# Rows of two time blocks accumulated by state group in four PSUM tiles, one spectrum overlapped on VectorE, one input tile without its TensorE fix-up, and three scans' scaled states on ScalarE

## The chip, the cores and the metric

The kernel runs on one core of a Trainium2 chip. The metric is the device time of one execution in microseconds (us); lower is better. The engines that matter are TensorE (PE in the profile: matrix products into PSUM), VectorE (DVE), ScalarE (ACT), GpSimd (POOL, which here issues the DMAs that add what they carry to their destination) and SyncE (SP, which issues the plain loads, the transposing loads and the stores). Each engine works through its own list of instructions in order.

## What is computed

Two sequence mixers over the same `x` (2048 steps, 1024 channels) are blended by a gate. Cut to what matters:

```
g  = sigmoid((x * gate_w).sum(-1))
# A: diagonal complex state space, 1024 states
h[t] = Lam_bar * h[t-1] + B_bar x[t];   a = 2 Re(C h) + x * Dskip
# B: short filter over k, times v, then a long convolution
kv = shift(k) * v;   y = irfft(rfft(kv) * rfft(ssm_k)) + kv * ssm_D;   b = x * y
out = g * a + (1 - g) * b
```

`x` and all weights are bf16, the output is bf16.

## The kernel before

**First half, the convolution (to about 217 us).** Channels are taken in eight chunks `c` of 128. For a chunk, `fwd_K` (line 542) makes the spectrum of the filter and `fwd_V` (558) that of the data by matrix products with cosine and sine tables, ScalarE moves both from PSUM to SBUF (`Kh`, `Vh` in the profile), `products` (571) multiplies them on VectorE into `G`, and `inverse` (621) turns `G` back on TensorE (`psz`) and sends the result to a scratch in DRAM (`cv_scr`). The sequence is cut into four blocks; in `fwd_K` each block's spectrum gets the spectrum of the block before it added by 16 matmuls of 384 columns in all (lines 553 to 555).

**Second half, the states.** Time is cut into four blocks `tb` of 512 steps, states into four groups `g` of 256. `Bu(i)` (686) is the input product of the pair `order[i] = (tb, g)`, in two halves of 16 matmuls of 512 columns. A pair is either *plain* (`Bu_plain`, 736; the product of even and odd steps, `both` in the profile) or a *tile* (`Bu_tile`, 710; `odd` and `even` apart, with `lamd` matmuls that add Lambda times the odd half). For a plain pair `turn_U` (752) does that addition later: six ScalarE instructions into two `Q` tiles and two adding DMAs from POOL. Some input products are already mixed into the first half (the generator `tiles`, line 961).

`scan` (763) is VectorE's part for one pair: scan number `j = 4 tb + g`. It rotates the input (`A`, `trn`), runs four scan instructions (`W`), rotates back (`hb`, the odd-step states), then makes `q = lam * hb` (line 811, four scalings) and adds it to `U` (lines 813 to 815, the even-step states). `advance(j)` (1191) runs the middle of scan `j`, the first instruction of scan `j+1`, then the end of scan `j`; a `product` is done in the middle, after the second `trn`.

An output *row* `k` is a tile of 128 steps (`k = 4 tb + tl`). `loads(k)` (827) fetches the convolution's result `pbb` and `x` (`xr`); `scale_b(k)` (841) scales `pbb` by `1-g` on ScalarE, makes `gd = g * Dskip` there, and POOL adds `gd` to `pbb` by DMA; `product(k)` (875) multiplies `xr` by `pbb` on VectorE; `Cy` (1164) is the output product, 32 matmuls of 512 columns over all four groups in one PSUM tile (`psy`), followed by `scale_a` (869) on ScalarE; `combine(k)` (879) is an adding DMA of `xr` into that result, and `store(k)` (882) sends it out. PSUM is a ring of four tiles of 4 KB per partition.

**What sets the order.** Everything is emitted by hand, and `put` (92) keeps each engine's instructions in the order in which they are emitted. For each scan `j` the loop (1209) emits, in turn: the loads due, `advance(j)`, the VectorE part of the C matrix's scaling, the first half of a `turn_U`, the units of `plan[j]` (line 1174: `B9` is an input product, `C4` a row), the second half of that `turn_U`, and a `scale_b`. After the loop rows 12 to 15 are accumulated group by group, with group 3 last.

Of the kernel before, what the change touches and what calls it, by code (L numbers as in the profile page):

```python
# [20 lines left out]
def kernel(  # L21
# [75 lines left out]
    def mm(o, l, r, first, last):  # L97
        put("pe", nc.tensor.matmul, o, lhsT=l, rhs=r, start=first, stop=last)
# [18 lines left out]
    def act(o, i, **kw):  # L117
        put("act", nc.scalar.activation, out=o, in_=i, **kw)
# [423 lines left out]
    def fwd_K(c, fis=range(NFI)):  # L542
        eo = eos["k", c]
        if c not in KH:
            KH[c] = spectrum("K", c)
        for fi in fis:
            fsl = slice(fi * 128, (fi + 1) * 128)
            ps = ps2([128, 2, 4, 128], "psk")
            for cc in range(2):
                tab = CF if cc == 0 else SF  # L550
                for mt in range(2):
                    mm(ps[:, cc], tab[:, mt, fsl], eo[:, cc, mt], mt == 0, False)
                for mt in range(2):
                    tb2 = (SF, NCF)[cc][:, mt, fsl]
                    mm(ps[:, cc, 1:4], tb2, eo[:, 1 - cc, mt, 0:3], False, mt == 1)
            act(of_tile(KH[c], fi), ps, func=ACT.Copy)

    def fwd_V(c, fis=range(NFI)):
        eo = eos["v", c]
# [126 lines left out]
    def Bu(i):  # L686
        tb, g = order[i]
        if i in (10, 11):
            if i == 10:
                s5p["u2"] = xt_pool.tile([128, 2, 2 * (4 * HB + 4)], BF16, name="U2", tag="xT")  # L690
            U = s5p["u2"][:, i - 10]
        else:
            shape = [128, 2 * (4 * HB + 4)]
            if i in (6, 7, 8, 15):
                U = u4(shape, BF16, "U")
            else:
                home = uu[0 if i in (0, 1, 13, 14) else 1] if i < 6 or i in (13, 14) else s5p["uu"]
                U = home.tile(shape, BF16, name="U")
        if i in (4, 5, 7) or i >= 8:
            V_, O_ = U[:, 0:4 * HB], U[:, 4 * HB:]  # L700
            V_ = V_.rearrange("p (c j t) -> p c j t", c=2, j=2)
            O_ = O_.rearrange("p (c j t) -> p c j t", c=2, j=2)
            Us[tb, g] = V_, O_[:, :, :, 2:]
            turns_U[i] = turn_U(g, V_, O_)
            return [Bu_plain(tb, g, V_, O_, j) for j in range(2)]
        U = U[:, 0:8 * HB].rearrange("p (a c j t) -> p a c j t", a=2, c=2, j=2)
        Us[tb, g] = U[:, 0], U[:, 1]
        return [Bu_tile(tb, g, U, j, (i, j) == (2, 1)) for j in range(2)]
# [43 lines left out]
    def turn_U(g, V_, O_):  # L752
        both = slice(0, 2)
        for part in (((both, both, lam[:, 0]),), ((0, 1, lam[:, 1]), (1, 0, mlam))):
# [5 lines left out]
            gather(V_, Q)  # L760
            yield

    def scan(tb, g, fin):


        last = tb == NTB - 1 and g == NG - 1
        Ve, Uo = Us[tb, g]
        A = w2([128, 2, 2, HB], BF16, "A")
        W = None

        for js in ([slice(0, 1), slice(1, 2)] if last else [slice(0, 2)]):
            g2 = slice(2 * g + js.start, 2 * g + js.stop)
            full = [128, 2, js.stop - js.start, HB]
            Aj, Uj = A[:, :, js], Ve[:, :, js]
            tt(Aj, bc(TC[:, g2][:, None], full), Uj, ALU.mult)
            if js.start == 0:
                yield
            b = w2([128, 2, 2, HB], BF16, "trn")[:, :, js]
            tt(b, bc(TS[:, g2][:, None], full), Uj, ALU.mult)
            if js.start == 0:  # L780
                if g == 0 and tb > 0:
                    carry(tb)
                step(fin)
            tt(Aj[:, 0], Aj[:, 0], b[:, 1], ALU.add)
            tt(Aj[:, 1], Aj[:, 1], b[:, 0], ALU.subtract)
            if W is None:
                W = w2([128, 2, 2, HB], BF16, "W")
            for j in range(js.start, js.stop):
                pi = 2 * g + j
                for c in range(2):  # L790
                    put("dve", V.tensor_tensor_scan, out=W[:, c, j], data0=bc(rv2[:, pi:pi + 1], [128, HB]),
                        data1=A[:, c, j], initial=0.0 if tb == 0 else init[tb][:, c, pi:pi + 1],
                        op0=ALU.mult, op1=ALU.add)
            if js.start == 0:
                run(fin)
                hbs[tb, g] = s5p["hb"].tile([128, 2, 2, HB], BF16, name="hb")
            hb = hbs[tb, g][:, :, js]
            Wj = W[:, :, js]
            tt(hb, bc(TC[:, g2][:, None], full), Wj, ALU.mult)
            if tb < NTB - 1:  # L800
                copy(WL[tb][:, :, g2], Wj[:, :, :, HB - 1])
            b = w2([128, 2, 2, HB], BF16, "trn")[:, :, js]
            tt(b, bc(TS[:, g2][:, None], full), Wj, ALU.mult)
            if not last:
                yield
            tt(hb[:, 0], hb[:, 0], b[:, 1], ALU.subtract)
            tt(hb[:, 1], hb[:, 1], b[:, 0], ALU.add)
            q = [w2([128, 2, 2, HB], BF16, "q") for k in range(2)]
            for k in range(2):
                for j in range(js.start, js.stop):  # L810
                    ts(q[k][:, :, j], hbs[tb, g][:, :, j], lam[:, k, 2 * g + j:2 * g + j + 1], None, ALU.mult)
            o, (q1, q2) = Uo[:, :, js], [x[:, :, js] for x in q]
            tt(o, o, q1, ALU.add)
            tt(o[:, 0], o[:, 0], q2[:, 1], ALU.subtract)
            tt(o[:, 1], o[:, 1], q2[:, 0], ALU.add)

    ios, gas = {}, {}

# [8 lines left out]
    def loads(t_):  # L827
        if t_ >= NT - 4:
            if t_ == NT - 4:
                ios["last"] = xt_first.tile([128, 4, D], BF16, name="xlast", tag="xT")  # L830
            pbb, xr = bt_row(1, t_ - NT + 4), ios["last"][:, t_ - NT + 4]
        elif t_ in (3, 4, 8, 9):
            pbb, xr = (bt_row(0, 2 * ((t_ - 3) % 5) + k) for k in range(2))
        else:
            pbb = s5p["io"].tile([128, D], BF16, name="pbb", bufs=3)
            xr = s5p["io"].tile([128, D], BF16, name="xr", bufs=3)
        move(pbb.rearrange("p (c d) -> p c d", d=128), cv_scr[:, :, t_ % 4, t_ // 4].rearrange("c p d -> p c d"))
        move(xr, rows_of(xf, t_))
        ios[t_] = pbb, xr
# [70 lines left out]
    def run(gen):  # L910
        for _ in gen:
            pass
# [50 lines left out]
    for c in range(NC - 1):  # L963
# [66 lines left out]
        step(prod)  # L1030
        run(fk)
        run(prod)
        if nn < NC:
            tv = times_v(nn)
            step(tv)
        bu = [next(tiles) for _ in range({1: 1, 2: 1, 3: 1, 5: 1, 6: 2}.get(c, 0))] + [none, none]
        if c == 5:
            bu[1] = ahead = next(tiles)
        step(bu[0])
# [10 lines left out]
        fwd_V(n, (2, 3))  # L1050
        if bu[1] is not ahead:
            step(bu[1])
        if c == 2:
            lam_diag(1, lam_pool)
        old = tabs
# [43 lines left out]
    with tc.tile_pool(name="fin", bufs=1, side="right") as fin:  # L1099
# [7 lines left out]
        run(old)  # L1107
        steps(prod, 3)
        run(back)
        b0, b1, b2, b3 = tiles  # L1110
        run(b0)
        gate(1)
        run(b1)
        run(prod)
        lam_diag(2, lam_pool, True)
        run(b2)
        run(b3)
        gate(2)
        b6, b7 = Bu(6)
        step(b6)  # L1120
        steps(turning[0], 2)
        step(b7)
        step(b6)
        back = inverse(c)
        step(back)
        step(b7)
        run(back)
        steps(turning[1], 2)
    h3.close()
# [41 lines left out]


    NS = NTB * NG
    plan = ["B8", "B9 B10", "B11", "B12 C0", "C1", "C2", "C3", "B13 B14", "C4 B15", "C5", "C6", "C7", "C8", "C9", "C10", "C11"]
    turned = dict(zip(range(3, 12), (8, 9, 4, 10, 11, 12, 13, 14, 15)))
    turned[0] = 7
    rows = dict(scaled=0)

    def between(j):
        for unit in plan[j].split():  # L1180
            if unit[0] == "C":
                product(int(unit[1:]))
        yield

    def prepare():
        scale_b(rows["scaled"])
        rows["scaled"] += 1

    scans = [scan(j // NG, j % NG, between(j)) for j in range(NS)]

# [4 lines left out]
        run(scans[j])  # L1195

    def Cy_row(k):
        if k + 3 < NT - 4:
            loads(k + 3)
        if k > 0:  # L1200
            store(k - 1)
        Cy(k // NG, k % NG)
        combine(k)
        if 0 < k < NT - 6:
            prepare()

    Bu_next(7)
    step(scans[0])
    for j in range(NS):
        if 10 <= j < 14:  # L1210
            loads(j + 2)
        advance(j)
        for t in turning[2 * j:2 * j + 2]:
            run(t)
# [1 line left out]
        turn = turns_U[turned[j]] if j in turned else none  # L1216
        step(turn)
        for unit in plan[j].split():
            (Bu_next if unit[0] == "B" else Cy_row)(int(unit[1:]))
        run(turn)  # L1220
        if j == 5:
            run(turns_U[5])
        if j < 3:
            prepare()
        if 11 <= j < 15:
            scale_b(j + 1)
        if j == 0:
            load_xT(3)
            loads(2)
        if j == 8:  # L1230
            gate(3)

    store(NT - 5)
    tb = NTB - 1
    t0 = tb * 4
    pss = []
# [44 lines left out]
```

## Time and profile before

| | |
|---|---|
| median of 3 runs | 399.38 us (399.07 to 400.0) |
| the profiled execution | 399.34 us, of which the span of the core is 397.3 us |
| granted TensorE clock | 0.997 |
| TensorE | 387.4 us busy (97% of the span), 2493 matmuls |
| VectorE | 378.3 us (95%), 616 instructions |
| ScalarE | 279.4 us (70%), 420 instructions |
| GpSimd | 70.8 us (18%), 95 instructions |

Times inside the profile count from the start of the span; the 2.0 us between span and run lie around it. Nearly every instruction stands under line 94, the line of `put`, so the groups are read by the names of the tiles: `psy<-CT,hb` is an output product, `xr<-xr,pbb` and `BT<-BT` (128x1024, VectorE) are products of rows for rows whose two buffers lie in the spent matrix `BT` (3, 4, 8 and 9).

### The profile page before, as it was taken

What the parts mean: (1) busy time and instruction counts of PE and PEld (TensorE: products, weight loads), DVE (VectorE), ACT (ScalarE), POOL (GpSimd) and SP (SyncE); (2) the same over time, 40 slices, a digit from 0 to 9 for tenths busy, and PEclk for the clock granted to TensorE, in tenths of its full rate; (3) what the DMA queues carried; (4) which work ended last, traced back from release to release, by engine and by line L of the source; (5) the groups of instructions that cost most, each with busy time, mean ns of one, the idle gap of its engine ahead of it and who ended that gap; (6) DMA issues with size and microseconds to landing.
All of it is one profiled execution on the core that took longest, in us unless ns stands there. A gap on an engine that the chain in (4) does not pass through costs nothing.

```text
span 397.3 us, 6652 instructions
## 1 busy us (share of the span) xinstructions
PE 387.4 (97%) x2493; PEld 210.8 (53%) x2493; DVE 378.3 (95%) x616; ACT 279.4 (70%) x420; POOL 70.8 (18%) x95
## 2 busy tenths in 40 slices
PE   8999899999999999999999999999999999999995
PEld 5456357474656648567557444444444444444442
DVE  8799999999999999999999999999999999999974
ACT  4797995979879796765455689957995668974001
POOL 3011030200303011020000001413442333541000
PEclk9999999999999999999999999999999999999998
DMA  7869996996929389068994699898999869998302
GB/s 160 160 139 209 204 221 131 222 225 126 222 52 226 68 150 196 27 134 108 173 204 102 166 171 229 166 197 157 217 183 193 178 146 203 245 244 202 75 26 106
DMA packets 129313, 65.19 MB, mean 164 GB/s; under 512 B 106361, under 2 KB 113281, under 8 KB 129282
## 3 DMA queue, kind: packets, MB, share of 16 engines
q1 hardware_dynamic: 117664, 42.22, 48.8%
q0 software_dynamic: 11536, 22.55, 33.2%
q8 instruction: 19, 0.31, 0.3%
q14 instruction: 12, 0.10, 0.1%
q10 hardware_dynamic: 82, 0.02, 0.0%
HBM read 12.86 MB, written 8.39 MB: 53 GB/s over the span
## 4 chain that ended last, share of the span: by engine, by line
PE 82%; DVE 9%; ACT 6%; issue 2%; POOL 0%; DVEq 0%; POOLq 0%; ACTq 0%
PE psy L94 28%; PE both L94 19%; PE psk L94 9%; PE psz L94 5%; PE taps L94 5%; PE even L94 5%; PE odd L94 4%; DVE BT L94 3%; PE psv L94 3%; PE foldk L94 3%; ACT Vh L94 2%; DVE wkh L94 2%; DVE G L94 1%; PE p L94 1%; DVE t L94 1%
## 5 line engine op out<-in xcount | busy, mean ns | idle before, releaser
L94 PEld LDWEIGHTS <-BT 128*128 128x128 bf16 x672 | 65.4, 98 | 45.2
L94 PE MATMUL both<-xT,BT 128*128 128x512 bf16 x352 | 76.8, 379 | 0.0
L94 PE MATMUL psy<-CT,hb 128*128 128x512 bf16 x256 | 56.6, 379 | 0.0
L94 PE MATMUL psy<-CT,U 128*128 128x512 bf16 x256 | 56.4, 379 | 0.0
L94 PEld LDWEIGHTS <-U 128*128 128x128 bf16 x256 | 25.0, 98 | 30.2
L94 PEld LDWEIGHTS <-hb 128*128 128x128 bf16 x256 | 25.0, 98 | 30.0
L94 ACT ACTIVATE Vh<-psv 128x1024 bf16<-128x1024 f32 x32 | 31.0, 1034 | 11.5 <-PE psv L94 11.5
L94 ACT ACTIVATE U<-both 128x512 bf16<-128x512 f32 x44 | 24.2, 594 | 17.3 <-PE both L94 17.2
L94 POOL DMA_DIRECT2D U<-Q x22 | 19.2, 942 | 89.7 <-ACT U L94 51.8
L94 DVE TENSOR_TENSOR_SCAN W<-rv,init,A 128x256 bf16<-128x256 f32 x48 | 32.2, 732 | 0.0
L94 PE MATMUL taps<-dg,kT 128*128 128x128 bf16 x512 | 31.0, 222 | 0.0
L94 POOL DMA_DIRECT2D G<-wkh x8 | 9.7, 1218 | 115.7 <-DVE wkh L94 115.7
L94 PEld LDWEIGHTS <-kT 128*128 128x128 bf16 x512 | 29.6, 99 | 1.0 <-DMA kT<-in_B_k_dram 0.3
L94 PE MATMUL psk<-eok,SF 128*128 128x512 bf16 (+1 forms) x128 | 29.4, 352 | 0.0
L94 PEld LDWEIGHTS <-SF 128*128 128x128 bf16 x192 | 18.8, 98 | 19.9 <-issue 0.8
L94 PE MATMUL psz<-G,CI 128*128 128x512 bf16 x64 | 24.3, 380 | 2.4 <-DVE G L94 1.9
L94 ACT ACTIVATE BT<-psy,gcols 128x1024 bf16<-128x1024 f32 x5 | 5.6, 1114 | 29.9 <-PE psy L94 29.9
L94 ACT ACTIVATE Q<-U,lam 128x512 bf16<-128x512 bf16 (+1 forms) x44 | 25.5, 607 | 0.0
L94 PE MATMUL psz<-G,SI 128*128 128x512 bf16 x64 | 24.3, 379 | 0.0
L94 DVE TENSOR_TENSOR U<-U,q 128x512 bf16<-128x512 bf16 (+2 forms) x51 | 23.5, 488 | 0.6
L94 DVE TENSOR_TENSOR wkh<-BT,Vh 128x3072 bf16<-128x3072 bf16 (+4 forms) x20 | 21.8, 1111 | 0.0
L94 DVE TENSOR_TENSOR wkh<-Kh,Vh 128x3072 bf16<-128x3072 bf16 (+2 forms) x16 | 21.3, 1352 | 0.0
(179 smaller groups left out, 776.4 us busy)
## 6 DMA issues: line engine op xcount, KB each, us to landing
U<-Q POOLq DMA_DIRECT2D x22, 256.0 KB, 5.0
G<-wkh POOLq DMA_DIRECT2D x6, 768.0 KB, 7.8
cv_scr<-cv SPq DMA_DIRECT2D x16, 256.0 KB, 2.8
v<-in_B_v_dram SPq DMA_DIRECT2D x3, 1024.0 KB, 9.8
pbb<-cv_scr SPq DMA_DIRECT2D x8, 256.0 KB, 4.7
xr<-in_A_x_dram SPq DMA_DIRECT2D x8, 256.0 KB, 4.6
pbb<-gd POOLq DMA_DIRECT2D x8, 256.0 KB, 6.6
BT<-cv_scr SPq DMA_DIRECT2D x8, 256.0 KB, 6.6
```

Of the source, the lines that this page charges most:

```text
L94: i = f(*a, **kw)
```

## The change

Four things are changed together.

1. *Last kernel spectrum.* For chunk 7 `fwd_K` leaves out the 16 matmuls of 384 columns, and `overlap_K` does the same six additions in place on VectorE, after the products of chunk 6.
2. *Pair 6 plain.* Pair 6 (block 0, group 2) becomes plain. Its eight `lamd` matmuls and the table `lamd2` (six ScalarE instructions) go; a `turn_U(6)` comes, run whole just ahead of input product 7. One half of pair 4 moves from the last chunk's stage to the end of the stage before it.
3. *Rows of blocks 1 and 2 by groups.* `Cy_group(tb, g)` does group `g` of all four rows of a block, in four PSUM tiles that are held through the four groups. The plan, the loads, the scalings of `pbb`, the products and the stores have new due times.
4. *q by ScalarE.* For scans 12, 13 and 14 the four scalings of `q` become ScalarE instructions, emitted at the end of iteration `j` ahead of its `scale_b`; the three additions to `U` follow in the next scan, after its scan instructions.

```diff
@@ fwd_K
-                    mm(ps[:, cc], tab[:, mt, fsl], eo[:, cc, mt], mt == 0, False)
-                for mt in range(2):
+                    mm(ps[:, cc], tab[:, mt, fsl], eo[:, cc, mt], mt == 0, c == NC - 1 and mt == 1)
+                for mt in range(0 if c == NC - 1 else 2):
...
+    def overlap_K(c):
+        K = KH[c][0]
+        for b in (3, 2, 1):
+            tt(K[:, 0, b], K[:, 0, b], K[:, 1, b - 1], ALU.add)
+            tt(K[:, 1, b], K[:, 1, b], K[:, 0, b - 1], ALU.subtract)
@@ Bu
-        if i in (4, 5, 7) or i >= 8:
+        if i in (4, 5) or i >= 6:
@@ scan
+            while put_off:
+                put_off.pop()[1]()
             if js.start == 0:
                 run(fin)
...
-            q = [w2([128, 2, 2, HB], BF16, "q") for k in range(2)]
-            ...
+            by_act = tb == NTB - 1 and not last
+            if by_act:
+                q = [s5p["Q"].tile([128, 2, 2, HB], BF16, name="Q") for k in range(2)]
+            else:
+                q = [w2([128, 2, 2, HB], BF16, "q") for k in range(2)]
+            def scaled(q=q):
+                for k in range(2):
+                    for j in range(js.start, js.stop):
+                        a = (q[k][:, :, j], hbs[tb, g][:, :, j], lam[:, k, 2 * g + j:2 * g + j + 1])
+                        if by_act:
+                            act(a[0], a[1], func=ACT.Identity, scale=a[2])
+                        else:
+                            ts(*a, None, ALU.mult)
+            def summed(q=q, js=js):
+                ...
+            if by_act:
+                put_off.append((scaled, summed))
@@ loads
-        elif t_ in (3, 4, 8, 9):
+        elif t_ in (3, 4, 8):
...
+        elif t_ in (9, 10):
+            if t_ == 9:
+                ios["two"] = xt_pool.tile([128, 4, D], BF16, name="xtwo", tag="xT")
+            pbb, xr = (ios["two"][:, 2 * (t_ - 9) + k] for k in range(2))
@@ stage of chunk 6 (c == 6, n == 7) and last stage
         run(prod)
+        if n == NC - 1:
+            overlap_K(n)
...
-        bu = [next(tiles) for _ in range({1: 1, 2: 1, 3: 1, 5: 1, 6: 2}.get(c, 0))] + [none, none]
+        bu = [next(tiles) for _ in range({1: 1, 2: 1, 3: 1, 5: 1, 6: 3}.get(c, 0))] + [none, none]
...
+        run(bu[2] if c == 6 else none)
...
-        b0, b1, b2, b3 = tiles
+        b0, b1, b2 = tiles
...
-        lam_diag(2, lam_pool, True)
         run(b2)
-        run(b3)
         gate(2)
         b6, b7 = Bu(6)
-        step(b6)
+        run(b6)
         steps(turning[0], 2)
-        step(b7)
-        step(b6)
+        run(b7)
         back = inverse(c)
@@ the loop over scans
-    plan = ["B8", "B9 B10", "B11", "B12 C0", "C1", "C2", "C3", "B13 B14", "C4 B15", "C5", "C6", "C7", "C8", "C9", "C10", "C11"]
+    plan = ["B8", "B9 B10", "B11", "B12 C0", "C1", "C2", "C3 B13", "B14 B15", "G10", "G11", "G12 G13", "G20", "G21",
+            "G22 G23", "", ""]
...
+    multiplied = {3: (0,), 4: (1,), 5: (2,), 6: (3,), 8: (4,), 9: (5, 6), 10: (7,), 11: (8,), 12: (9, 10), 13: (11,)}
+    loaded = {7: (7,), 8: (8,), 9: (9,), 10: (10,), 11: (12, 11), 12: (13, 14), 13: (15,)}
+    scaled_b = {0: (0,), 1: (1,), 2: (2,), 4: (3,), 5: (4,), 6: (5,), 7: (6,), 8: (7,), 9: (8,), 10: (9,), 11: (10,),
+                12: (11, 12), 13: (13, 14), 14: (15,)}
+    stored = {11: range(4, 8), 14: range(8, 12)}
     def between(j):
...
+        for k in multiplied.get(j, ()):
+            product(k)
...
+    def Cy_group(tb, g):
+        if g == 0:
+            end_late()
+            four[tb] = [ps2([128, 2, 512], "psy") for tl in range(4)]
+        for tl in range(4):
+            ps, k = four[tb][tl], tb * 4 + tl
+            Cy_g(tb, tl, [ps[:, 0], ps[:, 1]], g, g == NG - 1)
+            if g == NG - 1:
+                scale_a(k, [(slice(0, D), flat(ps))])
+                combine(k)
+    run(turns_U[6])
     Bu_next(7)
...
         run(turn)
...
-        if j < 3:
-            prepare()
-        if 11 <= j < 15:
-            scale_b(j + 1)
+        if put_off:
+            put_off[-1][0]()
+        for k in scaled_b.get(j, ()):
+            scale_b(k)
...
-        if j == 8:
+        if j == 7:
             gate(3)
```

Below, G13 means group 3 of block 1, "scan 12" the scan with `j = 12`, and a "unit" 32 matmuls of 512 columns (an input product of a pair, a row, or a group of four rows).

## The prediction

> **What bounds it now.** I read the busy shares first, then the chain of work that ended last, then VectorE's timeline at the end.
>
> ```profile
> PE 387.4 (97%) x2493; PEld 210.8 (53%) x2493; DVE 378.3 (95%) x616; ACT 279.4 (70%) x420; POOL 70.8 (18%) x95
> ```
>
> ```profile
> 316.74 76.01 PE psy L94 x352
> 392.75 0.03 issue
> ```
>
> ```profile
> 381.97 0.94 DVE L94 TENSOR_TENSOR U<-U,q 128x512 bf16<-128x512 bf16 x3
> 382.83 2.49 DVE L94 TENSOR_TENSOR xlast<-xlast,BT 128x1024 bf16<-128x1024 bf16 x4
> ```
>
> TensorE and VectorE are both nearly full, but at the end TensorE is last: from 164.4 us the chain is TensorE alone to 392.75. 76.01 / 352 gives 0.216 us for a 512-column matmul, so a unit of 32 is 6.91. VectorE has scan 15's `hb` at 381.4 and its `U` at 382.8; TensorE's last unit starts at 385.7 (timeline), so VectorE is 4.3 us early. That is all the delay it may get for nothing, and the question for every edit.
>
> **1. Spectrum and pair 6, on TensorE.** In the chain eight 512- and eight 384-column matmuls of `psk` take 3.03 us; less 8 x 0.216 leaves 1.30, so 16 of them save 2.6. Pair 6's eight `lamd` matmuls save 0.9 (0.44 for four); its products cost the same (64 of 0.109 or 32 of 0.216). VectorE gets six additions of 128x512, at 0.335 from start to start (two `A<-A,trn` in 0.75) 2.1 us. They start after `G` of chunk 6 (188.34) and fill a gap:
>
> ```profile
> 189.70 2.29 DVE L94 TENSOR_TENSOR G<-Kh,Vh 128x4096 bf16<-128x4096 bf16 x1 [1.36 <-ACT Vh L94]
> ```
>
> `Vh` comes 2.6 us sooner, so the products start at 190.45, 0.75 later, and `G` of chunk 7 is there at 212.73 + 0.75 = 213.5. TensorE before it: `psz` of chunk 6 at 188.93 - 2.6 + 3.45 (the half of pair 4 put there) = 189.8, when `G` has long been ready; then six times 3.45 and two gates of 0.8 to 212.1. It waits 1.4 us for `G`. Input product 7 starts at 213.5 + 3.45 = 217.0 instead of 219.1. **So 3.5 us of work saved give 2.1.** ScalarE loses 1.75 (`lamd2`) and gets 2.8 (`turn_U(6)`); its gaps between 222 and 230 (0.4, 2.4, 0.8) hide that, and scan 2 reads the result only at 231.6. Without those gaps scan 2 would wait, VectorE first.
>
> **2. Groups, on TensorE.** The matmuls are the same. From 217.0, 13 units and a gate reach G10 at 307.6; G13 ends at 335.2, G23 at 362.8. Scan 4 was done at 274, so operands cost nothing. The fourth tile of G10 takes the gate's place in PSUM: ScalarE has the gate at about 311.9 (last input 307.95, `turn_U` 1.6, `scale_b(6)` 2.1), TensorE needs it at 312.7; 0.8 us of cover.
>
> **3. ScalarE's order ahead of row 10.** Before, `scale_b` of a row ran two scans ahead of its product. Now products 9 and 10 stand in scan 12, `scale_b(9)` and `(10)` at the ends of iterations 10 and 11, and ahead of both, in ScalarE's order, the four `scale_a` of G13, which wait for TensorE. Their prices:
>
> ```profile
> 334.90 0.50 ACT L94 ACTIVATE Q<-U,mlam 128x256 bf16<-128x256 bf16 x1
> 335.30 1.32 ACT L94 ACTIVATE Q<-U,lam 128x512 bf16<-128x512 bf16 x2
> 337.52 1.11 ACT L94 ACTIVATE m<-psy,gcols 128x1024 bf16<-128x1024 f32 x1 [0.90 <-PE psy L94]
> 338.54 1.14 ACT L94 ACTIVATE BT<-BT,omg 128x1024 bf16<-128x1024 bf16 x1
> 339.57 1.14 ACT L94 ACTIVATE gd<-rows,gcols 128x1024 bf16<-128x1024 bf16 x1
> ```
>
> From start to start: `scale_a` 1.0, `scale_b` 2.1, `turn_U` 1.2 and 1.6. G13 ends at 335.2; `scale_a(7)` to 336.4, second half of `turn_U(14)` 338.0, `scale_b(9)` 340.1, `turn_U(15)` 342.9, `scale_b(10)` 345.0; POOL issues 0.3 later, 345.3. How long such a DMA takes, issue to landing, depends on the traffic. The DMA views of 300 to 330 us, then 330 to 360:
>
> ```profile
> pbb<-gd POOLq DMA_DIRECT2D x2, 256.0 KB, 3.5
> ```
> ```profile
> pbb<-gd POOLq DMA_DIRECT2D x2, 256.0 KB, 8.7
> ```
>
> The ends are 3.3 and 9.3. At 345 the stores of rows 4 to 7, the loads of 13 to 15 and three gathers are under way, as in the second window: I take 7.5, landing 352.75. VectorE would be there at 343.64 (product 8 before) + 0.75 + 1.2 (two products more) + 0.6 (a short wait for row 6, scaled behind input product 15) = 346.2. **First wait, 6.6 us.** The additions to `A` of scan 12 start at 353.4 instead of 344.25.
>
> **4. q ahead of row 11.** Scan 12's `hb` is ready 6.0 us later, 359.4. Only then can ScalarE start the four scalings, and `scale_b(11)` is behind them: 3 x 0.61 + 0.71 = 2.5, then 2.1, then 0.3 to POOL, 364.35. Product 11 is the second instruction of scan 13; VectorE has 0.6 us of work before it. By then the loads are through; two such DMAs at 364 and 373 took 4.9 and 3.3, so I take 4: 368.35. **Second wait, 8.3 us.** VectorE's gain is 1.05 a scan, from the start of the scalings to that of the additions:
>
> ```profile
> 350.30 1.19 DVE L94 TENSOR_SCALAR q<-hb,lam 128x512 bf16<-128x512 bf16 x4
> 351.40 1.47 DVE L94 TENSOR_TENSOR U<-U,q 128x1024 bf16<-128x1024 bf16 x3
> ```
>
> It is spent in that wait. Behind q stand also `scale_b(12)` and the `scale_a` of G23, which free the PSUM tiles of the last block: `scale_a(8)` ends at 367.2, TensorE wants the tile at 362.8. But its third row needs `U` of scan 12, at 369.0 + 0.7 + 2.8 + 1.4 = 373.9, so that is late in any case. A rule speaks against this part: the Trainium skill (ScalarE: Activation LUTs, Rules for kernel authors) gives multiplications to VectorE, as the faster per element in bf16. The trace agrees (0.26 against 0.61 from start to start); by the rule, with q left on VectorE, the second wait would be 2.5 shorter for 1.05 of work.
>
> **5. To the end.** Product 11 ends at 369.0. Before, the same place was 354.0 and `U` of scan 15 came 28.83 later. Of that go the q of scans 13 and 14 (2.1) and products 10 and 11 (1.2); the sum of scan 12 comes in (1.4), and 0.4 of waiting for q of scan 14 (ScalarE 2.6 against 2.2 of VectorE's work). So `U` is there at 369.0 + 27.3 = 396.3, `hb` 1.4 sooner, 394.9. TensorE has reached the second half of the first row of the last group by 393.0, waits to 394.9, and ends 0.86 + 3 x 1.73 later, 401.0. VectorE has four products (2.5, to 398.8) and the finishing of rows 12 to 15 (1.2, 0.6, 1.2, 1.4 in its timeline): 403.2 against 394.2 before. **Sum: +9.0 us on the profiled execution's 399.34, so 408.3**; the median shown is 0.04 above that execution. SP: the load of row 11's `xr` waits for the gather of row 5 (about 338) and the stores and three rows' loads are behind it; row 11 needs it after 358, 20 us of cover, so nothing.
>
> The Trainium skill, DMA: Bandwidth & Descriptors, Anatomy of one DMA, SWDGE path, fits 2.0 us plus bytes / 436e3 to a DMA issued by GpSimd; an estimate from it is 2.6 us for 256 KB. No such DMA here took less than 3.3. By it the waits would shrink by 4.9 and 1.4 and the sum be 402.0, still slower and next to the second rival, with whose chance I count it.
>
> **Rivals.**
> - *TensorE stays last (faster, 397.2).* If VectorE's waits at products 10 and 11 stay under its slack, the 2.1 us of part 1 are the result. Without waits `hb` of scan 15 would be at 381.4 + 0.75 - 3.15 = 379.0, and TensorE would need it at 384.5: 5.5 us of room, 7.6 until the time before is reached. For it: DMAs of 3.3 us exist. Against: the second wait alone is 2.5 + 2.1 + 0.3 + 3.3 - 0.6 = 7.6 at the shortest, and it follows from the order alone. The point from which it decides: both waits together under 7.6.
> - *Only the second wait (401.7).* Row 10 lands before 346.2. `U` of scan 15 would be at 389.7, VectorE's last instruction at 396.6, +2.4. For it: the quiet 3.5. Against: even that lands at 348.8.
> - *Row 11's DMA meets traffic too (412.6).* The gather for row 12 is right behind it and the stores may run late; at 8.3 instead of 4 the sum grows by 4.3.
>
> **Numbers.** Forecast 0.68, only the second wait 0.12, traffic 0.10, TensorE last 0.10. The landing at row 10 between 3.3 and 9.3 moves the sum by -4.2 and +1.8, that at row 11 between 3.3 and 8.3 by -0.7 and +4.3: 403.4 at the low end of the forecast. The range takes in the second rival and the third: 401 to 412.6, and leaves out the first. A measurement here can tell 0.2% (0.8 us) from no change. Faster 0.09, within 0.2% 0.04, slower 0.87.
>
> **What would show it.** VectorE's timeline in scan 12 and 13: an idle stretch ahead of the product of row 10 (some 6 us, near 347 to 353) and of row 11 (some 8, near 360 to 368). ScalarE's q ahead of `scale_b(11)`. TensorE's `psz` of chunk 7 waiting about 1.4 us for `G`, and input product 7 at 217. In the last blocks TensorE waiting for `U` and `hb`. The forecast is wrong if VectorE shows no idle time there, if TensorE is full to its end, or if input product 7 starts later than 219.

## The result, and the profile after

| | |
|---|---|
| median of the changed kernel | 419.91 us (415.8 to 421.43, 6 runs) |
| the kernel before beside it | 399.45 us (399.07 to 400.97, 6 runs) |
| ratio | 1.0487, 95% interval 1.0434 to 1.0541 |
| the profiled execution after | 421.43 us, span 419.7 us, granted clock 0.978 |

The change makes the kernel 20.5 us slower; the forecast was 9.0, and 419.9 is above the range. The first part of the page, and its slices of the span (40 slices of 10.5 us; one digit is the busy share in tenths):

```profile
PE 387.6 (92%) x2401; PEld 206.0 (49%) x2437; DVE 376.9 (90%) x610; ACT 287.1 (68%) x432; POOL 72.3 (17%) x98
...
PE   7999899999999999999989599899999999955984
...
DVE  8689999999999999999999499999998999065996
...
PEclk9899999999999999999999899999999999995999
```

VectorE is 1.4 us less busy than before. TensorE is as busy as before (0.2 more), although matmuls worth 3.5 us were taken out, because some of the others ran at a lower clock (below). The span is 22.4 longer, and the rows show where: a hole near 235 us (PE 5, DVE 4), and one from 357 to 388 (DVE 0, then PE 5 and 5) that ends with a clock digit of 5. The first hole was not forecast.

**The first half** came as forecast. VectorE's timeline shows the six additions and the products right behind them; TensorE's shows the wait for `G` (in brackets: idle time before, and what ended it), 1.39 against a forecast of 1.4. In the seven executions below that have the same first half it is 0.88 to 1.41:

```profile
190.02 2.34 DVE L94 TENSOR_TENSOR Kh<-Kh 128x512 bf16<-128x512 bf16 x6
192.28 2.28 DVE L94 TENSOR_TENSOR G<-Kh,Vh 128x4096 bf16<-128x4096 bf16 x1
```
```profile
215.45 0.38 PE L94 MATMUL psz<-G,CI 128*128 128x512 bf16 x1 [1.39 <-DVE G L94]
```

This execution began 1.9 us late, from its first loads on (TensorE waits 2.27 us for one of them, 0.60 before; the same `psz` starts at 213.4 to 214.0 in ten of the executions below). That much of its times is no effect of the change.

**The hole at pair 6**, in the timeline of all engines:

```profile
223.71 0.86 POOL L94 DMA_DIRECT2D U<-Q  x1 [48.49 <-DVE q L94]
...
235.37 0.86 POOL L94 DMA_DIRECT2D U<-Q  x1 [10.80 <-DMA U<-Q]
235.91 0.44 POOL L94 MEMSET U<- 128x4 bf16 x1
...
236.38 1.57 ACT L94 ACTIVATE U<-both 128x512 bf16<-128x512 f32 x3 [11.37 <-POOL U L94]
237.52 8.68 PE L94 MATMUL both<-xT,BT 128*128 128x512 bf16 x32 [4.64 <-ACT U L94]
...
239.74 0.69 DVE L94 TENSOR_TENSOR A<-TCS,U 128x1024 bf16<-128x1024 bf16 x1 [5.48 <-DMA U<-Q]
```

Read it downwards. The first of `turn_U(6)`'s two adding DMAs is issued at 223.71 and takes 11.1 us to land. The second waits for it on POOL, and behind the second stands a clearing of 0.44 us for the next pair's `U`. ScalarE, which is to write that `U` from PSUM, waits 11.4 us for the clearing; TensorE finds no free PSUM tile, 4.64; VectorE's scan 2 waits for the second DMA, 5.48.

**The two waits at products 10 and 11**, again by the timeline. First ScalarE's and POOL's part in product 10:

```profile
347.78 1.14 ACT L94 ACTIVATE xtwo<-xtwo,omg 128x1024 bf16<-128x1024 bf16 x1
...
353.71 1.14 ACT L94 ACTIVATE gd<-rows,gcols 128x1024 bf16<-128x1024 bf16 x1
...
359.19 0.86 POOL L94 DMA_DIRECT2D U<-Q  x1 [6.63 <-DMA U<-Q]
359.73 1.20 POOL L94 DMA_DIRECT2D xtwo<-gd  x1
367.63 0.69 DVE L94 TENSOR_TENSOR xtwo<-xtwo 128x1024 bf16<-128x1024 bf16 x1 [10.83 <-DMA xtwo<-gd]
```

`scale_b(10)` ends at 354.85, but its addition is issued at 359.73: on POOL it stands behind the second half of `turn_U(15)`, which waits for the landing of the first. It lands 7.9 us after its issue. Then product 11:

```profile
374.33 2.56 ACT L94 ACTIVATE Q<-hb,lam 128x512 bf16<-128x512 bf16 x4 [19.48 <-issue]
...
379.26 0.86 POOL L94 DMA_DIRECT2D pbb<-gd  x1 [18.33 <-ACT gd L94]
380.95 4.09 ACT L94 ACTIVATE BT<-psy,gcols 128x1024 bf16<-128x1024 f32 x4
...
382.10 6.31 PE L94 MATMUL psy<-CT,hb 128*128 128x512 bf16 x16 [9.55 <-ACT BT L94]
382.59 0.69 DVE L94 TENSOR_TENSOR xr<-xr,pbb 128x1024 bf16<-128x1024 bf16 x1 [7.74 <-DMA pbb<-gd]
```

ScalarE starts `q` when `hb` of scan 12 is there, and row 11 comes behind it: 7.74 us of waiting. Meanwhile TensorE has no free PSUM tile for 9.55 us, since the four `scale_a` of G23 that free them (380.95) stand behind `q` and two rows' scalings; its next 16 matmuls take 6.31 instead of 3.62.

**The end.** VectorE is last, and TensorE waits for it:

```profile
408.11 2.76 PE L94 MATMUL psy<-CT,hb 128*128 128x512 bf16 x12 [1.31 <-DVE hb L94]
...
409.68 2.49 DVE L94 TENSOR_TENSOR xlast<-xlast,BT 128x1024 bf16<-128x1024 bf16 x4
```

### The profile page after: what moved, and what is told of

The parts are those of the page before. It is cut to its first block, busy times and chain, and to the rows that moved or that the text cites. A ratio compares the mean times of both kernels' runs of the same rounds, so it can differ in the third digit from the quotient of the medians.

```text
span 419.7 us, 6516 instructions
## 1 busy us (share of the span) xinstructions
PE 387.6 (92%) x2401; PEld 206.0 (49%) x2437; DVE 376.9 (90%) x610; ACT 287.1 (68%) x432; POOL 72.3 (17%) x98
## 5 line engine op out<-in xcount | busy, mean ns | idle before, releaser
L94 PE MATMUL both<-xT,BT 128*128 128x512 bf16 x375 | 85.2, 384 | 5.1 <-ACT U L94 4.6
L94 PEld LDWEIGHTS <-BT 128*128 128x128 bf16 x640 | 62.6, 98 | 53.9 <-issue 7.1
L94 PE MATMUL psy<-CT,hb 128*128 128x512 bf16 x250 | 59.9, 392 | 12.4 <-ACT BT L94 9.6
L94 ACT ACTIVATE U<-both 128x512 bf16<-128x512 f32 x48 | 26.3, 594 | 31.9 <-PE both L94 20.3
L94 POOL DMA_DIRECT2D U<-Q x24 | 22.3, 941 | 112.5 <-DVE q L94 48.5
L94 ACT ACTIVATE Vh<-psv 128x1024 bf16<-128x1024 f32 x32 | 31.0, 1034 | 11.4 <-PE psv L94 9.6
L94 PE MATMUL psk<-eok,SF 128*128 128x512 bf16 (+1 forms) x118 | 27.7, 354 | 0.3
L94 ACT ACTIVATE Q<-U,lam 128x512 bf16<-128x512 bf16 (+1 forms) x48 | 27.4, 606 | 0.0
L94 ACT ACTIVATE Q<-hb,lam 128x512 bf16<-128x512 bf16 x12 | 7.7, 710 | 25.9 <-issue 25.0
L94 ACT ACTIVATE cv<-psz 128x1024 bf16<-128x1024 f32 x16 | 16.5, 1033 | 5.4 <-PE psz L94 5.4
```

What stands on the lines that cost most here:

```text
L94: i = f(*a, **kw)
```

## The experiments

Theory C at first: the loss is three separate things, the hole at pair 6 and the two waits, and the parts' prices add up. The rivals are in the expectations. Times are medians; the kernel before gave 399.3 to 399.5 beside each call.

**One part undone at a time.**

*x1, pair 6 a tile again* (its `lamd` matmuls and table return, `turn_U(6)` goes):

```diff
-        if i in (4, 5) or i >= 6:
+        if i in (4, 5, 7) or i >= 8:
...
-    run(turns_U[6])
```

> Pair 6 as a tile again, with its lamd table and matmuls; the other three parts stay. Theory C (a chain of waits): in the changed kernel the first addition of the input tile of pair 6 takes 11.1 us to land among the loads of C, POOL's second addition waits for it, the small memset behind that holds ScalarE for 11.4 us, and TensorE comes to G10 some 8 us late; everything behind G13 (the scaling of row 10, product 10) is late by as much. So 420 falls by 7 to 8, less 0.9 of matmuls: 412 to 414. Rival R (the two long waits of VectorE swallow it): 419 to 421.

411.61 us, ratio 1.0302 [1.0282, 1.0322]: 8.3 less, and the hole is gone from all three engines; products 10 and 11 still wait (8.6 and 7.7). So the hole is pair 6's.

*x2, q back on VectorE:*

```diff
-            by_act = tb == NTB - 1 and not last
+            by_act = False
```

> q of scans 12 to 14 back on VectorE, in its old place; the other parts stay. Theory C: the wait ahead of product 11 (7.7 us) loses the 2.5 us of ScalarE's q but VectorE has 1.05 more work ahead of it in scan 12 and in each of the next two: 418 to 419.5. Rival R2 (q is what makes that wait): most of 7.7 goes, 412 to 414.

415.39 us, 1.0407 [1.0377, 1.0436]: 4.5 less, between the two. The wait at product 11 goes wholly, not by the 2.5 of C: without `q` in its way ScalarE reaches `scale_b(11)` before scan 12 has its state. 7.7 less the 3.15 that VectorE's list grows by (3 x 1.05, the forecast's gain a scan) is 4.55.

*x3, rows one at a time again* (the plan, loads, scalings and products of before; the other three parts stay):

```diff
...
-            "G22 G23", "", ""]
+    plan = ["B8", "B9 B10", "B11", "B12 C0", "C1", "C2", "C3", "B13 B14", "C4 B15", "C5", "C6", "C7", "C8", "C9", "C10", "C11"]
...
```

> Rows of blocks 1 and 2 one after the other, with the old plan, loads, scalings, products and stores; spectrum, plain pair 6 and q on ScalarE stay. Theory C: rows 10 and 11 are scaled two scans ahead again, so both long waits go; what is left is TensorE's loss at pair 6: 403 to 407. Rival R3 (the loss at pair 6 is hidden by slack): 397 to 399.

410.01 us, 1.0242 [1.0197, 1.0286]: 9.9 less. No product waits, and the hole at pair 6 stays. The expectation missed a new wait: TensorE stands 4.00 us for a PSUM tile, since the `scale_a` that would free it now stands behind `q` on ScalarE. So `q` there makes a wait with either order of rows; what it costs with this one was not measured apart.

*x4, the spectrum on TensorE again:*

```diff
-        if n == NC - 1:
-            overlap_K(n)
```

> The last spectrum whole on TensorE, no additions on VectorE; the other three parts stay. Theory C: TensorE reaches the inverse of chunk 7 about 1.2 us later and VectorE 2.3 us of additions sooner; the chain at the end hangs on G13, so 421 (420 to 422.5). Rival R4 (VectorE's time at the start of the scans decides): 417 to 419.

420.32 us, 1.0516 [1.0497, 1.0535]: inside the change, where VectorE is last, the spectrum's saving is 0.4 us, too little to be told from none.

**What makes the hole at pair 6.**

*x5, the turn later:*

```diff
-    run(turns_U[6])
     Bu_next(7)
+    run(turns_U[6])
```

> The turn of U(6) is issued after the input products of pair 7 have been set going instead of ahead of them; everything else as in the changed kernel. Theory C (the added transfer of U(6) lands 11 us after its issue because of the traffic, and everything behind it waits): the landing stays at 10 to 11 us, VectorE's scan 2 still waits for it about 5 us (5.5 before this edit), only the wait of ScalarE's writing of U(7) behind the clearing on GpSimd goes, and with it TensorE's 4.6 us: 415 to 418 us. Rival O (it is the order on GpSimd that costs, the clearing of U(7) behind the waiting transfer): the hole around pair 6 goes wholly, as where pair 6 was turned by TensorE: 411 to 413 us. A third outcome, that the later issue makes scan 2 later still, gives 420 us or more.

419.16 us, 1.0471 [1.0417, 1.0525], not to be told from the changed kernel. Neither theory: TensorE's 4.64 are gone, as O said, and the first DMA, issued at 227.14, lands in 4.7 us, not 11; but scan 2 still waits 4.27, and TensorE loses 3.6 us at row 0 instead, in four waits for the scaled C.

*x6, C loaded without transposing:*

```diff
-        load_CT(pi)
+        for c, src in enumerate((A_C_re, A_C_im)):
+            move(CT[pi][:, c], src[pi * 128:(pi + 1) * 128, :])
```

> The loads of C for pairs 4 to 7 do not transpose: same rows, plain copies of the same bytes, so that the values of C in those four pairs are other ones; all else is the changed kernel. Theory C (the transposing loads that run beside it make the added transfer of U(6) take 11 us): it lands in 3.5 to 5 us, scan 2 does not wait for it or by under 1 us, TensorE's 4.6 us shrink to 0 to 1, C is there in time: 411 to 414 us, and the two waits at products 10 and 11 (10.8 and 7.7 us on VectorE) stay. Rival T (the transfer is slow by its own kind, adding on the way, or by its own queue): landing 9 to 11 us as before, time 418 to 421 us.

418.74 us, 1.0463 [1.0427, 1.0499]. Both fall, though the time is in T's range: the DMA lands in 7.3 us, and the eight executions with transposing loads and the turn in its place show 7.2 to 11.1. Plain loads alone do not bring it to C's 3.5 to 5; one execution can't show whether transposing adds to the rest. TensorE's wait shrinks to 0.8, and again 3.3 come back at row 0.

*x12, pair 6 plain in the kernel before, alone* (with the half of pair 4 moved and the `lamd2` table gone, as in the change):

```diff
-        if i in (4, 5, 7) or i >= 8:
+        if i in (4, 5) or i >= 6:
...
+    run(turns_U[6])
```

> The kernel before with part 2 of the change alone: pair 6 plain, with its turn ahead of input product 7. Theory C (TensorE is last in the kernel before, so what TensorE loses decides: 0.7 to 4.6 us for U(7) behind the clearing on GpSimd and 1.2 to 3.6 for the scaled C at row 0, less 0.9 of saved matmuls; VectorE's 2.3 to 5.5 us behind the late addition meet its 4.3 us of room): 402 to 405 us, and the sum of the two losses about the same in each execution, since a shorter first one comes back at row 0. Rival M (the hole costs what it cost inside the whole change, 8 us): 406 to 408 us.

407.14 us, 1.0186 [1.0159, 1.0213]: the 8 of rival M. TensorE is last in this kernel, and these lines give the price that C had missed (the first row in the timeline of before; then the timeline of x12, whose last row is cut by the window's end; then its windows, where the column after POOL is the granted clock):

```profile
260.55 13.98 PE L94 MATMUL psy<-CT,hb 128*128 128x512 bf16 x64
```
```profile
237.03 30.70 PE L94 MATMUL both<-xT,BT 128*128 128x512 bf16 x128 [4.00 <-ACT U L94]
267.57 7.72 PE L94 MATMUL psy<-CT,hb 128*128 128x512 bf16 x35
```
```profile
235.00:240.00 5.00, 2.97 (x8) 1.01 (x8) 0.28 (x1) 4.04 (x9) 1.15 (x3) 0.61 1.13 204
240.00:245.00 5.00, 5.00 (x18) 1.98 (x17) 4.89 (x13) 4.97 (x9) 0.57 (x1) 0.70 1.21 193
245.00:250.00 5.00, 5.00 (x25) 2.26 (x24) 4.61 (x8) 4.97 (x9) 0.89 (x2) 1.00 1.26 230
```

After 4.0 us of idling the clock is at 0.61 and 0.70 for two windows of 5 us. From the start of the 128 matmuls behind it to that of the first row it is 30.54 us, where 128 x 0.216 is 27.65. Wait 4.0 and clock 2.9 are 6.9; the first row starts 7.0 later than before (267.57 against 260.55).

**What makes the two waits.**

*x7, rows 9 and 10 earlier* (`loaded` and `scaled_b` of row 10 at iteration 9):

```diff
@@ loaded
-    9: (9,), 10: (10,),
+    9: (9, 10),
@@ scaled_b
-    9: (8,), 10: (9,), 11: (10,),
+    9: (8, 9, 10),
```

> The loads of rows 9 and 10 are issued together one iteration earlier for row 10, and their scalings go to ScalarE at the end of iteration 9, ahead of the output scalings of group 3 of block 1. Theory C (the 10.8 us at product 10 come from ScalarE's order: the scaling of row 10 behind four output scalings that wait for TensorE): the wait at product 10 goes, product 11 still waits because its scaling stands behind the q of the scan, which waits for the state: this second wait grows by what the first one had covered, to 9 to 14 us, and the time is 413 to 417 us. Rival D (the transfer of the row is what is late, for traffic): product 10 still waits 4 us or more and the time is 418 to 421 us. Rival S (both waits are one queue, the second vanishes with the first): 408 to 411 us.

408.34 us, 1.0206 [1.016, 1.0253]: 11.6 less, more than C said. The time is in the range of rival S, whose mechanism falls all the same: product 10 doesn't wait, and the wait at 11 stays 7.74; it neither goes nor grows. It follows from the order within one scan (`hb`, `q`, scaling, DMA), so whatever came before it shifts it and covers none of it.

*x8, row 11 as well*, on top of x7 (the edit scales it at the end of iteration 11, one later than the expectation has it):

```diff
@@ scaled_b
-    12: (11, 12),
+    11: (11,), 12: (12,),
```

> As the run with rows 9 and 10 earlier, and in addition the scaling of row 11 at the end of iteration 11's predecessor instead of behind the q. Theory C: no wait of VectorE at a product from row 8 on is over 1 us, the hole around pair 6 (about 9 us) stays, so that 399.4 + 7.8 for the hole - 2 for the spectrum + up to 3 for TensorE's later waits give 404 to 408 us. Rival L (the later groups themselves cost, by PSUM or by TensorE's clock after the holes): 410 to 415 us.

404.39 us, 1.011 [1.0076, 1.0143]: C by its time, but not by its waits: 4.16 of the second are left, since row 11's addition still stands behind the second half of `turn_U(15)` on POOL (issued at 357.38 and 357.91). The hole stays. Its DMA landed early here, in 7.2 us, TensorE waited only 0.71 for PSUM, and then this, at row 0 (TensorE's timeline, then the windows):

```profile
264.60 0.59 PE L94 MATMUL psy<-CT,hb 128*128 128x512 bf16 x2 [1.00 <-DMA CT<-Q]
266.44 0.59 PE L94 MATMUL psy<-CT,hb 128*128 128x512 bf16 x2 [1.25 <-DMA CT<-Q]
268.43 11.90 PE L94 MATMUL psy<-CT,hb 128*128 128x512 bf16 x42 [1.40 <-DMA CT<-Q]
```
```profile
265.00:270.00 5.00, 2.35 (x7) 0.75 (x6) 4.93 (x13) 2.63 (x6) 1.39 (x2) 0.70 1.11 228
270.00:275.00 5.00, 5.00 (x16) 1.87 (x15) 4.93 (x12) 2.11 (x4) 0.70 (x1) 0.61 0.05 8
```

The waits are 3.65. The 42 matmuls run from 268.43 to 280.16, where the next group starts: 11.73, less 42 x 0.216, is 2.7 for the clock. With the 0.71 that is 7.1, so the hole's price is nearly the same by either way.

*x13, one swap in the changed kernel:*

```diff
+        if j == 11:
+            for k in scaled_b.pop(j):
+                scale_b(k)
         run(turn)
```

> The changed kernel with one swap: in iteration 11 the scaling of row 10, and with it its addition on GpSimd, is emitted ahead of the second half of the turn of U(15) instead of behind it. Theory G (GpSimd's order: the addition of row 10 was ready at 354.8 and stood 4.6 us behind the second half, which waited for the landing of the first): the addition is issued at about 353.3 instead of 359.7 and lands 5 to 8 us later, the wait at product 10 falls from 10.8 to 3 to 5.5 us, the one at product 11 stays at 7.7, and 5.5 to 8 us go: 412 to 414.5 us. Rival A (the addition takes as long as the traffic lasts, to about 365 to 368 us whenever it is issued): product 10 still waits over 8 us, 417.5 to 420.5 us.

411.07 us, 1.0306 [1.0286, 1.0325]: G, and somewhat more. The wait at product 10 is 3.17, that at 11 stays 7.73 (POOL's timeline, then VectorE's):

```profile
349.58 0.86 POOL L94 DMA_DIRECT2D xtwo<-gd  x1 [0.99 <-ACT gd L94]
355.03 0.86 POOL L94 DMA_DIRECT2D U<-Q  x1 [4.60 <-DMA U<-Q]
```
```profile
357.29 0.69 DVE L94 TENSOR_TENSOR xtwo<-xtwo 128x1024 bf16<-128x1024 bf16 x1 [3.17 <-DMA xtwo<-gd]
```

The addition still takes 7.7 us to land, so its issue, and not its transfer, was what POOL's order held back.

**What is left when they are mended.**

*x9, all but plain pair 6, with rows 6, 9, 10 and 11 scaled earlier* (x1 and x8 together, and):

```diff
@@ scaled_b
-    6: (5,), 7: (6,),
+    6: (5, 6),
```

> All of the change but the plain pair 6, with the scalings of rows 6, 9, 10 and 11 each moved ahead (row 6 to the end of iteration 6, 9 and 10 to that of iteration 9, 11 to that of iteration 11). Theory C (the loss is the two waits at products 10 and 11, the 3 us at product 6 and the pair's hole, and nothing else): no wait of VectorE at a product is over 1 us, TensorE is full to its end, and what is left is the spectrum's 2.6 us less the 0.6 that TensorE waits for G: 397.0 to 398.3 us, faster than both kernels. Rival L (holding four PSUM tiles, or q on ScalarE, costs by itself): 400 to 404 us.

398.39 us, 0.9969 [0.9955, 0.9983]: 1.0 us faster than the kernel before, though not as C had it: in the profiled execution, the slowest of the twelve (400.15), product 11 still waits 6.20 and VectorE is last. The 400 to 404 of L did not come, but TensorE does wait 1.53 us at the first group of block 2.

*x10, the same with q on VectorE* (the edit of x2 on top of x9):

> As the run before it, with q of scans 12 to 14 on VectorE again. Theory C (q on ScalarE only shortens VectorE's list, by 2.1 to 3.2 us, and VectorE had 4.3 us to spare before the change): TensorE stays last, 397.0 to 398.5 us, the same within 0.2%. Rival Q (VectorE is last once TensorE is 2 us earlier and two products more stand in scan 12): 0.8 to 3 us slower than with q on ScalarE.

399.2 us, 0.9991 [0.9977, 1.0005]: 0.8 slower than x9, the low end of Q. With the waits mended, `q` on ScalarE seems to gain: an execution of x9 is the faster one in 122 of the 144 pairs, though the intervals overlap.

*x14, x9 with the swap of x13* (the same three lines):

> The mended kernel (all but the plain pair 6, with the scalings of rows 6, 9, 10 and 11 earlier) with the same swap in iteration 11, where it puts the addition of row 11 ahead of the second half of U(15). Theory G (the 6.2 us that VectorE still waited at product 11 were that addition, behind the second half on GpSimd): the wait goes or is under 2 us, VectorE is no longer last, TensorE is, and the time is that of part 1 alone: 397.0 to 397.9 us. Rival A (traffic holds the addition): the wait stays over 4 us and the time at 398.0 to 398.8 us. Rival H (the second half of U(15), now later, is what scan 15 waits for): VectorE waits for U ahead of scan 15, 398 to 400 us.

398.3 us, 0.9981 [0.9963, 1.0]. G was right on the mechanism: no product of scan 12 or 13 waits, and TensorE is last. It was wrong on the size, and the time is in A's range. ScalarE's timeline, then TensorE's:

```profile
333.84 1.15 ACT L94 ACTIVATE gd<-rows,gcols 128x1024 bf16<-128x1024 bf16 x1 [5.18 <-DMA BT<-gd]
334.89 1.32 ACT L94 ACTIVATE Q<-U,lam 128x512 bf16<-128x512 bf16 x2
336.12 4.10 ACT L94 ACTIVATE m<-psy,gcols 128x1024 bf16<-128x1024 f32 x4
```
```profile
337.26 3.61 PE L94 MATMUL psy<-CT,hb 128*128 128x512 bf16 x16 [1.34 <-ACT m L94]
```

ScalarE stands 5.18 for a `gd` buffer that row 8's addition still reads; behind it are the four `scale_a` of G13, whose tiles TensorE needs for the first group of block 2, and waits 1.34 for.

*x11, the spectrum by VectorE in the kernel before, alone* (the hunk of `fwd_K`, `overlap_K` and the half of pair 4, of the change's diff):

```diff
+        if n == NC - 1:
+            overlap_K(n)
```

> The kernel before with part 1 of the change alone: the last spectrum's sixteen matmuls replaced by six additions on VectorE, and the half of pair 4 moved. Theory C: 2.6 us of TensorE go, 0.6 of them come back as its wait for G, VectorE's first scans start no later than input product 7 lets them: 397.2 to 398.3 us (ratio 0.994 to 0.997). Rival V (VectorE, 2.1 us longer, passes the delay to G and on to the scans, so that nothing is gained): 399.2 to 400.5 us.

397.45 us (397.29 to 397.89), 0.9944 [0.9923, 0.9965]: C, 1.9 us faster, the best version found. TensorE is last to the end; its closing stretch of 352 output products has the length shown of before and starts 1.6 earlier (316.74 there):

```profile
315.13 76.01 PE psy L94 x352
```

## Why the prediction was wrong

The direction was right and so were most mechanisms; the step that failed is **step 1**, at "its gaps between 222 and 230 hide that, and scan 2 reads the result only at 231.6". It priced `turn_U(6)` by its six ScalarE instructions and left out its DMAs, though the prediction elsewhere gives such DMAs 3.3 to 9.3 us. Two of them in series from 223.7 are at 231.6 only if both are quick, and it named nothing that stands behind them on POOL. Measured: +7.8 us alone, 8.3 inside the change, instead of a saving; the forecast's 408.3 with that alone is above the range.

By parts: the spectrum alone -1.9 (x11), pair 6 alone +7.8 (x12), the groups +9.9 (x3), `q` +4.5 (x2). They sum to 20.3 against 20.5 measured, but that closeness is in part luck, for two prices are taken alone and two inside the change. With all four inside it (-0.4, 8.3, 9.9 and 4.5) the sum is 22.3. Executions of the changed kernel spread over 5.6 us, so whether the parts interact is not shown. The biggest term that the forecast left out is pair 6's hole; the second is POOL's order in step 3.

- *Step 1, the rest.* The spectrum's saving, its place and the 1.4 of waiting for `G` came as forecast.
- *Step 2.* The last input of `scale_a(7)`, forecast for 335.2, was there at 345.0. Of these 9.8 us 1.9 are the late start of this execution and nearly all the rest the hole: 4.64 of waiting for PSUM, about 1.6 for the clock behind it (29.23 us for 128 matmuls) and 1.28 of waiting for the scaled C at row 0. With the scalings moved the groups cost little: x9 and x14 hold them at 398.4 and 398.3. But they gain nothing either, for the spectrum alone gives 397.45 (x11); in x14 the 1.34 of TensorE's waiting is of the size of that loss. (The terms given for the gate, 307.95 + 1.6 + 2.1, make 311.65 and not 311.9; TensorE did not wait there.)
- *Step 3.* ScalarE's order came as written, and the landing took 7.9 (forecast 7.5). Its issue came 4.6 later than ScalarE allowed, because POOL's order was left out: the term "POOL issues 0.3 later". Wait 10.8 instead of 6.6; x13 shows that the swap alone takes most of it; there the scaling too stands ahead of the second half of `turn_U(15)` on ScalarE, which is 1.6 us.
- *Step 4.* 7.7 us against 8.3: right, with a landing of 3.3 against 4. Wrong was the sentence that `q` left on VectorE would shorten the wait by 2.5: it removes it (x2), because what row 11 waits for is not the length of `q` on ScalarE but its start, which waits for `hb`.
- *The two rules.* The Trainium skill's preference for VectorE in bf16 multiplications (ScalarE: Activation LUTs, Rules for kernel authors) holds in the kernel as changed, for a reason of order rather than speed (x2), and seems to fall in the mended one (x9 against x10). By the Trainium skill's fit for a GpSimd DMA (DMA: Bandwidth & Descriptors, Anatomy of one DMA, SWDGE path) the sum was 402.0; the trace does not agree, for the adding DMAs of 256 KB in the changed kernel took 3.3 to 11.1.
- *Step 5.* From the end of product 11 to `U` of scan 15: 26.5 against 27.3; the tail 6.7 against 6.9.

The profiled execution adds up: forecast 408.3; start 1.9; hole 7.9; POOL 4.6; landing of row 10 0.4; the second wait -0.6; the stretch to `U` -0.8; the tail -0.2. They make 421.5, and it took 421.43.

What stays open: which of the transfers under way (rows of the convolution, `x`, C) makes the first DMA of `turn_U(6)` take 7 to 11 us. Issued at 222 to 224 it lands between 229 and 235, and the one issued at 227.14 took 4.7 (x5). Plain loads of C left 7.3 (x6), so transposing alone is not the cause; the other transfers weren't tried one by one.

## What to carry to other kernels

When a step is moved or added, write down for every queue that it passes, the DMA-issuing engine's too, what stands behind its waiting instruction: here a clearing of 0.44 us and a row's addition, each held behind a landing, cost more than the 2.8 us of ScalarE's work that was priced. An instruction moved to a queue where it has to wait makes all that stands behind it there as late as that wait, so scalings that others need go ahead of it. And a hole in TensorE can be paid twice, in idle time and in the clock after it: here 4.0 and 2.9 us.

## What the runs showed of the hardware

An idle stretch of 4.0 us took the granted clock to 0.61 and 0.70 in the next two windows of 5 us (0.50 in windows of 1 us) and cost 2.9 us more (x12). The Trainium skill (TensorE: Matmul & The Clock Gate, Part 1: The HAM clock gate) says that the clock halves after an idle window of about 3.4 us, and this trace agrees. But three waits of 1.0 to 1.4 us within 5 us with two matmuls between each and the next, none of them as long as that window, did the same (0.70, 0.61; 2.7 us lost, x8), while a single wait of 1.39 or 1.28 in the changed kernel left the granted clock at 1.00. An adding DMA of 256 KB from GpSimd took between 3.3 us and 11.1 us in one execution, that of the changed kernel.
